# A streamed FFT filter and a Strassen-type gated projection on one core: where the sums of x's blocks, c22 and the filter step stand, which queue stores z, and when t is loaded

## Chip, core and metric

The kernel runs on one core of one Trainium2 chip. The metric is device time in microseconds (us) of one execution, given as the median of three runs. The engines are named as in the profile: PE is TensorE (its matmuls), PEld its weight loads, DVE VectorE, ACT ScalarE, POOL GpSimd, SP SyncE, which here does nothing but issue transfers.

## The reference

Two steps follow each other. `x` has 8 batches of 3072 tokens of 256 numbers, `d_ff` is 1536, all in f32.

```python
X = np.fft.rfft(x, axis=1)                     # along the 3072 tokens
y = np.fft.irfft(X * (filt_r + 1j * filt_i)[None], n=3072, axis=1)
t = y.reshape(8 * 3072, 256)
out = ((t @ w_a) * (t @ w_b)) @ w_out          # 256 -> 1536, 1536 -> 256
```

## The kernel before

**The two halves.** A main loop does the gated projection of batch b, and between its matmuls the Fourier filter of batch b+1 is streamed in. (The filter of batch 0 is done ahead of the loop, by the functions whose names begin with first_.) All matmuls on x's way take f32 numbers in two parts, a rounded part (xh, gh, yh, zh, ...) and the remainder (xl, gl, yl, zl), so that one product becomes three matmuls.

**The main loop.** A batch has 6 blocks c of 512 tokens, a block 6 pairs p of 256 columns of d_ff, so 36 pairs and 72 half pairs in a batch. A pair (function pair) forms both projections in 7 terms of 6 matmuls (term, L576 to L578) in place of 8, as Strassen's and Winograd's schemes do: sums of blocks of x and of the weights are multiplied, and sums of the terms give the blocks c11, c21, c22 and a21 of the result. The terms lie in the PSUM banks ps_p (two buffers, by turns from pair to pair), ps_q and ps_r. In program order: term 1 into ps_p, ScalarE copies it to s (L617); term 2 into ps_q, VectorE adds s and gives c11 (L621); term 5 into ps_r, copied to m5; term 6 on top of ps_p, copied to s; term 3 on top of ps_r, add with s gives c21 (L621); term 7 on top of ps_p, add with m5 gives c22 (L621); term 4 on top of ps_p again, from which a21 is copied (L654). Each of these overwrites or adds to a bank, and so waits for the copy or add that reads it. VectorE multiplies the two projections: L640 (c11 and c21), L645 (c22) and L655 (a21, straight from PSUM), into g. ScalarE casts g to gh (L584), GpSimd makes the remainder gl (L585), and the next pair multiplies both by w_out (project, L595 to L597, 24 matmuls in four places of the pair). A finished block is copied from PSUM and stored from the sync queue (store, L603). A pair has 42 + 24 = 66 matmuls.

**The hooks.** Twice in a pair, ahead of term 3 (half pair 2p) and ahead of term 4 (2p+1), `hooks` runs what a table, `plan`, names for this half pair. Its entries for a batch, by half pair, are:

- stage 1 of the next batch in 12 steps: load_x, load_s, split_x (L351, L352), s1 (6 matmuls at L360, then the cast zh L363 on ScalarE and the remainder zl L364 on VectorE), and store_z one half pair later (L369 to L372, issued from ScalarE's queue; a third store for the steps 8 to 11). One step every pair at half pairs up to 26; in batch 0 one step every half pair, from 12 on.
- the filter in 16 steps from half pair 29, one every pair: load_f and load_z (L391, L392, L398, from the sync queue, for the step after next), s2 (L407, L408; then on VectorE y at L418, two cross products at L420 into v, and y + v at L426), split_y (L433 on ScalarE, L434 on GpSimd) one half pair later, is1 (again L407, L408, copy to t, store to td from ScalarE's queue) three half pairs later.
- the last stage for the next block c+1: load_t (tt and gt, L531 and L533) at half pair 12c+2, is2 for each half of the columns (4 matmuls at L540, a copy to xf, L545) at 12c+4 and 12c+5, x_sums (four sums of x's blocks, L551) and x_parts (the casts xoh L560 and remainders xol L561) at 12c+6 and 12c+7. For the next batch's first block these are half pairs 65 to 70.

**What sets the order.** The program is scheduled by hand: each engine executes its instructions in the order of the code, and waits where its data or a buffer is not ready. s1, s2, is1 and is2 take by turns the two buffers of one PSUM pool (tag ff). Most SBUF tiles have one buffer: cs, g, s, m5, y, v, yh, yl, zh, zl, tt, gt and xf among them, so that the next use waits for the last reader of the use before. The core of a pair, from term 3 on:

```python
hooks(2 * p)
term(b, c, p, 3, rs)
add(1, rs, s)                         # c21, L621
nc.vector.tensor_tensor(out=g[:, 0]...)   # L640
term(b, c, p, 7, ps)
add(2, ps, m5)                        # c22, L621
...                                   # L645, project, parts
hooks(2 * p + 1)
term(b, c, p, 4, ps)
```

Of the kernel before, what the change touches and what calls it, by code (L numbers as in the profile page):

```python
# [14 lines left out]
ALU = mybir.AluOpType  # L15
# [181 lines left out]
def fft_filter_bilinear_kernel(ctx: ExitStack, tc, x, filt, fny, wa, wb, wo, s1c, gc, fc, fl, ic, sc, s1f, ff, fi, out):  # L197
# [168 lines left out]

    def store_z(b, i):
        zh, zl = held.pop(("zs", b, i))
        nc.scalar.dma_start(out=zd[b][0][:, 2 * i:2 * i + 2], in_=f32(zh))  # L369
        nc.scalar.dma_start(out=zd[b][1][:, 2 * i:2 * i + 2], in_=f32(zl))  # L370
        if i >= 8:
            nc.scalar.dma_start(out=zd[b][0][:, 2 * i + 8:2 * i + 10], in_=f32(zh))  # L372
# [39 lines left out]
    def s2(b, i):  # L412
        zt, fr, fm = held.pop(("z", b, i)), filts[2 * (i % 2)], filts[2 * (i % 2) + 1]
        ps = ps_f.tile([128, 2, D], F32, name="ps", tag="ff")
        turn(i, fct, flt, zt[:, 0], zt[0:96, 1], ps)
        y = later[0].tile([128, 2, D], F32, name="y", tag="y", bufs=1)
        v = later[0].tile([128, 2, D], F32, name="v", tag="v", bufs=1)
        nc.vector.scalar_tensor_tensor(out=y, in0=ps, scalar=sct[:, 0:1], in1=fr, op0=ALU.mult, op1=ALU.mult)  # L418
        for a in range(2):
            nc.vector.scalar_tensor_tensor(  # L420
                out=v[half[1 - a]], in0=ps[half[a]], scalar=sct[half[a], a:a + 1], in1=fm[half[1]],
                op0=ALU.mult, op1=ALU.mult,
            )
# [112 lines left out]
    def is2(b, c, k):  # L536
        tt, gt = held["t", b, c]
        ps = ps_f.tile([128, 4, N1], F32, name="ps", tag="ff")
        for n in range(4):
            nc.tensor.matmul(ps[:, n], tt[:, n, 128 * k:128 * k + 128], gt[:, n], start=True, stop=True)  # L540
        if k == 0:
            held["x", b, c] = moe[0].tile([128, 8, 256], F32, name="xf", tag="xf")
        else:
            del held["t", b, c]
        nc.scalar.copy(out=held["x", b, c][:, 2 * k:2 * k + 2].rearrange("p t n -> p (t n)"), in_=ps.rearrange("p n m -> p (n m)"))  # L545

    def x_sums(b, c):

        xf = held["x", b, c]
        for o, a, b_, op in ((4, 1, 0, ALU.subtract), (6, 3, 1, ALU.subtract), (5, 3, 4, ALU.subtract), (7, 2, 5, ALU.subtract)):  # L550
            nc.vector.tensor_tensor(out=xf[:, o], in0=xf[:, a], in1=xf[:, b_], op=op)  # L551

    def x_parts(b, c, part):
        xf = held["x", b, c]
        if part == 0:
            held["xo", b, c] = [p2.tile([128, 7, 256], F32R, name=t, tag=t) for t in ("xoh", "xol")]
        xh, xl = held["xo", b, c]
        for o, i in (((0, 1), (0, 1)), ((1, 3), (2, 4))) if part == 0 else (((3, 5), (4, 6)), ((5, 7), (6, 8))):
# [46 lines left out]
    def pair(u, last, hooks):  # L605

        b, c, p = u
        ps = ps_h.tile([128, 2, 256], F32, name="ps_p", tag="p", bufs=2)
# [11 lines left out]
        def add(n, bank, s):  # L620
            nc.vector.tensor_tensor(out=cs[:, :, n], in0=bank, in1=s, op=ALU.add)  # L621
# [15 lines left out]
        hooks(2 * p)  # L637
# [24 lines left out]


    with tc.manual_schedule():
# [53 lines left out]
        swap_front()  # L718
        is2(0, 0, 0)
        is2(0, 0, 1)  # L720
        x_sums(0, 0)
        x_parts(0, 0, 0)
        x_parts(0, 0, 1)

        last = None
        for b in range(B):
            plan = {}

            def at(slot, fn, *args):
                plan.setdefault(slot, []).append((fn, *args))  # L730
# [10 lines left out]
            if b + 1 < B:  # L741
# [89 lines left out]
```

## Time and profile before

| | us |
|---|---|
| runs | 2828.39, 2838.14, 2839.75 |
| median | 2838.14 |
| the profiled execution: time | 2827.78 |
| its span, first to last instruction | 2826.0 |
| PE busy in it | 2653.4 (94%) |
| DVE, ACT, POOL busy | 1755.6, 1409.0, 1401.5 (62, 50, 50%) |

Busy shares are means over the whole span, and its parts differ: the start and batch 0's stage 1 lie before 335 us, six batches between 335 and 2511 us, and from 2511 us on the last batch runs without a stream beside it. Matmuls overlap: a matmul's row lasts about 0.28 us, while one starts every 0.12 us. The granted clock is that of TensorE, as a share of full speed. A releaser in a row is what the profile infers to have ended a wait.

### The profile page before, as it was taken

How to read it: one execution, taken by the hardware profiler on the slowest of the kernel's cores; microseconds unless marked ns; L12 is line 12 of the kernel's file. 1: busy time of each engine (PE TensorE's matmuls, PEld its weight loads, DVE VectorE, ACT ScalarE, POOL GpSimd, SP SyncE). 2: the span in 40 equal slices, each digit the busy share in tenths (PEclk: the TensorE clock that was granted, in tenths of full speed). 3: DMA queues.
4: the chain of work that ended last, by engine and by line, in shares of the span. 5: the costliest groups of instructions: out<-in, count | busy, mean ns of one | idle time of the engine just before them, and what ended most of it. 6: DMA issues, size and time to landing. Idle time of an engine off the chain costs nothing.

```text
span 2826.0 us, 54174 instructions
## 1 busy us (share of the span) xinstructions
PE 2653.4 (94%) x20920; PEld 2541.0 (90%) x20920; DVE 1755.6 (62%) x2648; ACT 1409.0 (50%) x2630; POOL 1401.5 (50%) x1044
## 2 busy tenths in 40 slices
PE   4687899999999999999999999999999999999998
PEld 2387899998999999998999989999999999999998
DVE  5773576556855577455765567655785567754443
ACT  4443455554545555454555545555454545544443
POOL 3564454554544455454555545454464555544343
PEclk7889999999999999999999999999999999999999
DMA  7525342245413443244431445224441444310100
GB/s 241 160 89 170 120 149 85 79 140 148 134 47 133 139 125 114 74 139 124 135 113 64 137 136 147 64 98 159 122 127 47 146 135 127 109 31 20 38 20 16
DMA packets 213636, 310.89 MB, mean 110 GB/s; under 512 B 21393, under 2 KB 121298, under 8 KB 213330
## 3 DMA queue, kind: packets, MB, share of 16 engines
q1 hardware_dynamic: 156658, 227.46, 26.2%
q10 hardware_dynamic: 56720, 79.98, 8.3%
q8 instruction: 164, 2.69, 0.4%
q14 instruction: 94, 0.77, 0.1%
HBM read 202.49 MB, written 108.00 MB: 110 GB/s over the span
## 4 chain that ended last, share of the span: by engine, by line
PE 67%; DVE 21%; DMA 5%; issue 4%; ACT 2%; POOL 0%; SPq 0%; DVEq 0%; ACTq 0%; POOLq 0%
PE ps_p L576 8%; PE ps_p L578 7%; PE ps_p L577 7%; PE po L595 6%; PE po L597 6%; PE po L596 6%; DVE cs L621 6%; DVE g L640 4%; PE ps_r L576 4%; PE ps_r L578 4%; PE ps_r L577 4%; PE ps L540 3%; DVE xf L551 2%; DVE v L420 2%; PE ps_q L577 2%
## 5 line engine op out<-in xcount | busy, mean ns | idle before, releaser
L585 POOL TENSOR_TENSOR gl<-g,gh 128x512 fp32r<-128x512 f32 x576 | 784.8, 1362 | 1081.2 <-ACT gh L584 1038.6
L595 PE MATMUL po<-woh,gh 128*128 128x256 f32 x2304 | 650.1, 282 | 0.2 <-ACT gh L584 0.2
L596 PE MATMUL po<-wol,gh 128*128 128x256 f32 x2304 | 648.5, 281 | 0.0
L597 PE MATMUL po<-woh,gl 128*128 128x256 f32 x2304 | 647.4, 281 | 0.8 <-POOL gl L585 0.8
L584 ACT CAST gh<-g 128x512 fp32r<-128x512 f32 x576 | 358.1, 622 | 541.3 <-DVE g L640 380.3
L621 DVE TENSOR_TENSOR cs<-ps_r,s 128x512 f32<-128x512 f32 x288 | 198.9, 691 | 538.6 <-PE ps_r L578 502.8
L617 ACT COPY s<-ps_p 128x512 f32<-128x512 f32 x576 | 338.8, 588 | 317.3 <-PE ps_p L578 299.6
L597 PEld LDWEIGHTS po<-woh,gl 128*128 128x128 f32 x2304 | 437.2, 190 | 1.0 <-POOL gl L585 1.0
L595 PEld LDWEIGHTS po<-woh,gh 128*128 128x128 f32 x2304 | 436.6, 190 | 0.4 <-ACT gh L584 0.4
L596 PEld LDWEIGHTS po<-wol,gh 128*128 128x128 f32 x2304 | 435.8, 189 | 0.0
L576 PE MATMUL ps_p<-xoh,wah 128*128 128x256 f32 x1152 | 347.7, 302 | 70.1 <-DVE cs L621 50.5
L621 DVE TENSOR_TENSOR cs<-ps_q,s 128x512 f32<-128x512 f32 x288 | 199.2, 692 | 232.4 <-PE ps_q L578 210.8
L578 PE MATMUL ps_p<-xol,wah 128*128 128x256 f32 x1152 | 325.8, 283 | 0.3 <-POOL xol L561 0.3
L577 PE MATMUL ps_p<-xoh,wal 128*128 128x256 f32 x1152 | 325.7, 283 | 0.0
L576 PE MATMUL ps_p<-xoh,wbh 128*128 128x256 f32 x1152 | 325.5, 283 | 0.0
L577 PE MATMUL ps_p<-xoh,wbl 128*128 128x256 f32 x1152 | 324.9, 282 | 0.0
L578 PE MATMUL ps_p<-xol,wbh 128*128 128x256 f32 x1152 | 324.5, 282 | 0.0
L576 PEld LDWEIGHTS ps_p<-xoh,wah 128*128 128x128 f32 x1152 | 219.1, 190 | 111.8 <-DVE cs L621 92.3
L640 DVE TENSOR_TENSOR g<-cs 128x512 f32<-128x512 f32 x288 | 250.0, 868 | 32.8 <-POOL gl L585 2.6
L561 POOL TENSOR_TENSOR xol<-xf,xoh 128x256 fp32r<-128x256 f32 x192 | 246.5, 1304 | 17.5 <-ACT xoh L560 17.5
L434 POOL TENSOR_TENSOR yl<-y,yh 128x512 fp32r<-128x512 f32 x112 | 186.0, 1660 | 137.5 <-ACT yh L433 136.4
L578 PEld LDWEIGHTS ps_p<-xol,wah 128*128 128x128 f32 x1152 | 219.9, 191 | 0.6 <-POOL xol L561 0.6
(125 smaller groups left out, 6294.8 us busy)
## 6 DMA issues: line engine op xcount, KB each, us to landing
filt<-in_filt SPq DMA_DIRECT2D x336, 128.0 KB, 3.4
z<-zh ACTq DMA_DIRECT2D x112, 256.0 KB, 2.1
zt<-z SPq DMA_DIRECT2D x112, 256.0 KB, 3.1
td<-t ACTq DMA_DIRECT2D x128, 192.0 KB, 2.2
out<-ot SPq DMA_DIRECT2D x95, 256.0 KB, 2.1
tt<-td SPq DMA_DIRECT2D x47, 512.0 KB, 4.5
xt<-in_x SPq DMA_DIRECT2D x84, 256.0 KB, 2.8
st<-s1d SPq DMA_DIRECT2D x84, 256.0 KB, 3.5
```

What stands on the lines that cost most here:

```text
L561: nc.gpsimd.tensor_tensor(out=xl[:, o], in0=xf[:, i], in1=f32(xh[:, o]), op=ALU.subtract)
L576: nc.tensor.matmul(o, wh[:, p, w], xh[:, i], start=first and h == 0, stop=False, skip_group_check=True)
L577: nc.tensor.matmul(o, wl[:, p, w], xh[:, i], start=False, stop=False, skip_group_check=True)
L578: nc.tensor.matmul(o, wh[:, p, w], xl[:, i], start=False, stop=True, skip_group_check=True)
L584: nc.scalar.copy(out=gh, in_=g[:, f])
L585: nc.gpsimd.tensor_tensor(out=gl, in0=g[:, f], in1=f32(gh), op=ALU.subtract)
L595: nc.tensor.matmul(o, gh[:, ts], woh[:, n], start=n == 0 and j % 2 == 0, stop=False, skip_group_check=True)
L596: nc.tensor.matmul(o, gh[:, ts], wol[:, n], start=False, stop=False, skip_group_check=True)
L597: nc.tensor.matmul(o, gl[:, ts], woh[:, n], start=False, stop=n == NF - 1, skip_group_check=True)
L617: nc.scalar.copy(out=s, in_=bank)
L621: nc.vector.tensor_tensor(out=cs[:, :, n], in0=bank, in1=s, op=ALU.add)
L640: nc.vector.tensor_tensor(out=g[:, 0].rearrange("p (t n) -> p t n", t=2), in0=cs[:, 0, 0:2], in1=cs[:, 1, 0:2], op=ALU.mult)
```

## The change

1. **c22 first.** In pair the add of c22 stands ahead of the product L640 of before (L649 of after).
2. **Odd hooks.** hooks(2p+1) stand behind term 4 and its product (L661 of after), no longer ahead of term 4. The store at p = 1 stands behind term 6.
3. **The filter step in two places.** s2 keeps y and the first cross product. The second, the Nyquist row and y + v (sum_y) run in a new early hook, behind c11's add of the next pair.
4. **Sums of x's blocks.** x_sums is gone. is2 forms them: one operand is read from its PSUM bank, one in its first half, three in its second. is2 runs at half pairs 12c+5 and 12c+7, x_parts at 12c+8 and 12c+9 (for the next batch's first block 67, 69, 70, 71).
5. **t earlier.** load_t for a block runs at the half pair of the previous block's first x_parts, eight half pairs ahead of its is2; a batch's first block keeps two half pairs.
6. **z from the sync queue.** store_z issues on SyncE's queue. load_f goes one half pair later.

The diff, cut:

```diff
     def store_z(b, i):
-        nc.scalar.dma_start(out=zd[b][0][:, 2 * i:2 * i + 2], in_=f32(zh))
-        nc.scalar.dma_start(out=zd[b][1][:, 2 * i:2 * i + 2], in_=f32(zl))
+        nc.sync.dma_start(out=zd[b][0][:, 2 * i:2 * i + 2], in_=f32(zh))
+        nc.sync.dma_start(out=zd[b][1][:, 2 * i:2 * i + 2], in_=f32(zl))
...
         nc.vector.scalar_tensor_tensor(out=y, in0=ps, scalar=sct[:, 0:1], in1=fr, op0=ALU.mult, op1=ALU.mult)
-        for a in range(2):
-            nc.vector.scalar_tensor_tensor(
+        held["y", b, i] = y, v, ps, fm
+        cross(b, i, 0)
+
+    def sum_y(b, i):
+        cross(b, i, 1)
...
         nc.vector.tensor_tensor(out=y, in0=y, in1=v, op=ALU.add)
...
-    def x_sums(b, c):
+        for o, t, i in ((4, 1, 0),) if k == 0 else ((5, 1, 4), (6, 1, 1), (7, 0, 5)):
+            nc.vector.tensor_tensor(out=xf[:, o], in0=ps[:, t], in1=xf[:, i], op=ALU.subtract)
...
         add(0, qs, s)
+        hooks(early, 2 * p)
         term(b, c, p, 5, rs, True)
...
         add(1, rs, s)
+        term(b, c, p, 7, ps)
+        add(2, ps, m5)
         nc.vector.tensor_tensor(
...
-        term(b, c, p, 7, ps)
-        add(2, ps, m5)
...
         parts(u, 0)
-        hooks(2 * p + 1)
         term(b, c, p, 4, ps)
...
         nc.vector.tensor_tensor(out=g[:, 1, :256], in0=ps[:, 1], in1=a21, op=ALU.mult)
+        hooks(plan, 2 * p + 1)
...
                     at(t, s2, b + 1, i)
+                    early.setdefault(t + 1, []).append((sum_y, b + 1, i))
...
-                    t = 12 * c + 4 if c + 1 < NC else 67
-                    at(t - 2, load_t, nb, ncx)
+                    t = 12 * c + 5 if c + 1 < NC else 67
+                    if ncx == 0:
+                        at(t - 2, load_t, nb, 0)
                     at(t, is2, nb, ncx, 0)
-                    at(t + 1, is2, nb, ncx, 1)
-                    at(t + 2, x_sums, nb, ncx)
-                    at(t + 2, x_parts, nb, ncx, 0)
+                    at(t + 2, is2, nb, ncx, 1)
+                    if ncx + 1 < NC:
+                        at(t + 3, load_t, nb, ncx + 1)
+                    at(t + 3, x_parts, nb, ncx, 0)
```

VectorE's order in the middle of a batch, in a pair with a filter step, before (cs is written by the adds c21, c22 and, in the last row, c11 of the next pair):

```order
L621 TENSOR_TENSOR cs<-ps_r,s 128x2x256 [waits PE_49,Activation_49]
L640 TENSOR_TENSOR g<-cs 128x512 [waits DVE_49,Pool_49]
L621 TENSOR_TENSOR cs<-ps_p,m_15467 128x2x256 [waits PE_49]
L645 TENSOR_TENSOR g<-cs 128x256 [waits DVE_49]
L418 SCALAR_TENSOR_TENSOR y<-ps,sct,filt_93 128x512 [waits DMAHW6_49,DMAHW7_49,PE_49,Pool_49]
L420 SCALAR_TENSOR_TENSOR v<-ps,sct,filt_94 64x512 [waits DMAHW0_49]
L420 SCALAR_TENSOR_TENSOR v<-ps,sct,filt_94 64x512
L426 TENSOR_TENSOR y<-y,v 128x512 [waits DVE_49]
L655 TENSOR_TENSOR g<-ps_p,cs 128x256 [waits Activation_49]
L621 TENSOR_TENSOR cs<-ps_q,s 128x2x256 [waits DVE_49,PE_49,Activation_49]
```

And VectorE in the same place after:

```order
L627 TENSOR_TENSOR cs<-ps_r,s 128x2x256 [waits PE_49,Activation_49]
L627 TENSOR_TENSOR cs<-ps_p,m_19800 128x2x256 [waits PE_49]
L649 TENSOR_TENSOR g<-cs 128x512 [waits DVE_49,Pool_49]
L652 TENSOR_TENSOR g<-cs 128x256 [waits DVE_49]
L661 TENSOR_TENSOR g<-ps_p,cs 128x256 [waits Activation_49]
L418 SCALAR_TENSOR_TENSOR y<-ps,sct,filt_95 128x512 [waits DMAHW0_49,DMAHW7_49,PE_49,Pool_49]
L424 SCALAR_TENSOR_TENSOR v<-ps,sct,filt_96 64x512 [waits DMAHW1_49]
L627 TENSOR_TENSOR cs<-ps_q,s 128x2x256 [waits DVE_49,PE_49,Activation_49]
L424 SCALAR_TENSOR_TENSOR v<-ps,sct,filt_96 64x512
L434 TENSOR_TENSOR y<-y,v 128x512 [waits DVE_49]
```

c22's add moved up by one row, the product of a21 ahead of the filter's rows, and two of these behind c11's add of the next pair.

TensorE around the same s2 before, where po is the projection by w_out and ps_p the bank of terms 7 and 4:

```order
L597 MATMUL po<-woh,gl 128x256
L407 MATMUL ps<-zt,fct 128x512
L408 MATMUL ps<-zt,flt 128x512
L576 MATMUL ps_p<-xoh,wah 128x256
L577 MATMUL ps_p<-xoh,wal 128x256
```

And TensorE there after:

```order
L603 MATMUL po<-woh,gl 128x256
L582 MATMUL ps_p<-xoh,wah 128x256
L583 MATMUL ps_p<-xoh,wal 128x256
L584 MATMUL ps_p<-xol,wah 128x256
L582 MATMUL ps_p<-xoh,wbh 128x256
L583 MATMUL ps_p<-xoh,wbl 128x256
L584 MATMUL ps_p<-xol,wbh 128x256
L407 MATMUL ps<-zt,fct 128x512
L408 MATMUL ps<-zt,flt 128x512
```

s2's two matmuls moved from ahead of term 4 to behind it.

SyncE's queue between a batch's stage 1 and its first zt, before (after the last st load stand a block's stores, the filter's loads, t's and z's):

```order
L603 DMA out<-ot 128x512 [waits DMAHW0_49,Activation_49]
L391 DMA filt_93<-in_filt 64x512 [waits DMAHW1_49,DVE_49]
L391 DMA filt_93<-in_filt 64x512 [waits DMAHW3_49]
L392 DMA filt_94<-in_filt 64x512 [waits DMAHW5_49,DVE_49]
L391 DMA filt_95<-in_filt 64x512 [waits DMAHW7_49,DVE_49]
L391 DMA filt_95<-in_filt 64x512 [waits DMAHW0_49]
L392 DMA filt_96<-in_filt 64x512 [waits DMAHW1_49,DVE_49]
L531 DMA tt<-td 128x1024 [waits DMAHW2_49]
L533 DMA gt<-in_gc 128x512 [waits DMAHW3_49]
L398 DMA zt<-z_17797 128x2x256 [waits DMAHW6_49,DMAHW4_49]
```

And SyncE's queue there after:

```order
L609 DMA out<-ot 128x512 [waits DMAHW6_49,Activation_49]
L369 DMA z_13589<-zh 128x512 [waits DMAHW7_49]
L370 DMA z_13590<-zl 128x512 [waits DMAHW0_49,DVE_49]
L372 DMA z_13589<-zh 128x512 [waits DMAHW1_49]
L391 DMA filt_93<-in_filt 64x512 [waits DMAHW2_49]
L391 DMA filt_93<-in_filt 64x512 [waits DMAHW3_49]
L392 DMA filt_94<-in_filt 64x512 [waits DMAHW4_49]
L391 DMA filt_95<-in_filt 64x512 [waits DMAHW5_49]
L391 DMA filt_95<-in_filt 64x512 [waits DMAHW6_49]
L392 DMA filt_96<-in_filt 64x512 [waits DMAHW7_49]
L398 DMA zt<-z_13589 128x2x256 [waits DMAHW1_49,DMAHW0_49]
```

The last stage 1 step's three stores of z came in ahead of the filter's loads and the first zt, and tt and gt left this place.

## Rows read from the trace of the kernel before

**Rows 1.** The page's first part: engine, busy us, share of the span, instructions.

```profile
PE 2653.4 (94%) x20920; PEld 2541.0 (90%) x20920; DVE 1755.6 (62%) x2648; ACT 1409.0 (50%) x2630; POOL 1401.5 (50%) x1044
```

**Rows 2.** Stretch, us; busy (x) PE, PEld, DVE, ACT, POOL; clock; DMA share; GB/s.

```profile
210.00:335.00 125.00, 100.14 (x728) 95.90 (x727) 55.04 (x85) 50.20 (x98) 52.60 (x41) 0.90 0.46 150
```

**Rows 3.** The same view, a stretch in which TensorE does not wait.

```profile
1529.30:1539.60 10.30, 10.30 (x90) 10.30 (x89) 4.22 (x7) 5.58 (x10) 3.99 (x3) 1.00 0.47 159
```

**Rows 4.** Timeline of a pair without hook work: start, duration, instruction, [idle before <- releaser].

```profile
1516.44 0.69 DVE L621 TENSOR_TENSOR cs<-ps_r,s 128x512 f32<-128x512 f32 x1 [2.15 <-PE ps_r L578]
...
1517.85 0.68 DVE L621 TENSOR_TENSOR cs<-ps_p,m 128x512 f32<-128x512 f32 x1
...
1518.17 0.28 PE L597 MATMUL po<-woh,gl 128*128 128x256 f32 x1
...
1518.58 0.19 PEld L576 LDWEIGHTS ps_p<-xoh,wah 128*128 128x128 f32 x1 [0.33 <-DVE cs L621]
...
1518.82 0.28 PE L577 MATMUL ps_p<-xoh,wal 128*128 128x256 f32 x1
```

**Rows 5.** Waits of weight loads, 210 to 335 us: total, times, longest.

```profile
PEld ps_p L576 <- ACT s L617: 9.5, 4, 3.9
...
PEld ps L540 <- DMA tt<-td: 3.9, 1, 3.9
...
PEld ps_r L576 <- ACT m L617: 0.5, 1, 0.5
```

**Rows 6.** The same view, 335 to 2511 us.

```profile
PEld ps_p L576 <- DVE cs L621: 55.2, 109, 2.5
PEld ps_r L576 <- ACT m L617: 32.0, 50, 1.2
...
PEld ps L360 <- ACT xh L351: 0.2, 1, 0.2
```

**Rows 7.** The same view, 2511 to 2826 us.

```profile
PEld ps_p L576 <- DVE cs L621: 15.4, 31, 1.3
```

**Rows 8.** Timeline of a pair with a filter step.

```profile
1440.69 0.74 DVE L418 SCALAR_TENSOR_TENSOR y<-ps,sct,filt 128x512 f32<-128x512 f32 x1
...
1444.27 0.62 ACT L584 CAST gh<-g 128x512 fp32r<-128x512 f32 x1 [1.95 <-DVE g L655]
...
1445.42 0.38 PE L576 MATMUL ps_r<-xoh,wah 128*128 128x256 f32 x1 [0.43 <-ACT m L617]
```

**Rows 9.** Cast zh in batch 0; ScalarE's waits, 130 to 335; z's transfers.

```profile
222.99 0.59 ACT L363 CAST zh<-ps 128x512 fp32r<-128x512 f32 x1 [4.83 <-DMA z<-zh]
...
ACT zh L363 <- DMA z<-zh: 27.5, 9, 5.6
...
z<-zh ACTq DMA_DIRECT2D x112, 256.0 KB, 2.1
```

**Rows 10.** Matmuls' waits, 335 to 2511; a chain piece; the stretch behind it.

```profile
PE ps L540 <- DMA gt<-in_gc: 14.8, 7, 3.1
...
1637.34 5.89 DMA gt<-in_gc
...
1643.40:1647.60 4.20, 4.20 (x23) 4.20 (x24) 1.47 (x3) 0.59 (x1) 0.00 (x0) 0.60 0.24 54
```

**Rows 11.** Groups by line and shape: count, busy us, mean ns, idle before.

```profile
L551 DVE TENSOR_TENSOR xf<-xf 128x256 f32<-128x256 f32 x192 | 148.4, 811 | 16.1 <-ACT xf L545 14.4
L655 DVE TENSOR_TENSOR g<-ps_p,cs 128x256 f32<-128x256 f32 x288 | 122.1, 424 | 107.5 <-ACT cs L654 102.0
L561 POOL TENSOR_TENSOR xol<-xf,xoh 128x512 fp32r<-128x512 f32 x144 | 200.0, 1403 | 1.7 <-ACT xoh L560 1.7
L420 DVE SCALAR_TENSOR_TENSOR v<-ps,sct,filt 64x512 f32<-64x512 f32 x224 | 168.0, 750 | 5.2
L426 DVE TENSOR_TENSOR y<-y,v 128x512 f32<-128x512 f32 x112 | 86.9, 776 | 3.9
```

**Rows 12.** SyncE's issues ahead of a first zt.

```profile
1632.16 1.23 SPq L391 DMA_DIRECT2D filt<-in_filt  x2
```

More of the change, by code (lines that the diff above doesn't have):

```diff
@@ L368, in store_z @@
         zh, zl = held.pop(("zs", b, i))
[L369 to L370 removed]
+        nc.sync.dma_start(out=zd[b][0][:, 2 * i:2 * i + 2], in_=f32(zh))
+        nc.sync.dma_start(out=zd[b][1][:, 2 * i:2 * i + 2], in_=f32(zl))
         if i >= 8:
[L372 removed]
+            nc.sync.dma_start(out=zd[b][0][:, 2 * i + 8:2 * i + 10], in_=f32(zh))
     def load_tables():
@@ L418, in s2, with cross @@
         nc.vector.scalar_tensor_tensor(out=y, in0=ps, scalar=sct[:, 0:1], in1=fr, op0=ALU.mult, op1=ALU.mult)
-        for a in range(2):
-            nc.vector.scalar_tensor_tensor(
-                out=v[half[1 - a]], in0=ps[half[a]], scalar=sct[half[a], a:a + 1], in1=fm[half[1]],
-                op0=ALU.mult, op1=ALU.mult,
-            )
+        held["y", b, i] = y, v, ps, fm
+        cross(b, i, 0)
+    def cross(b, i, a):
+        _, v, ps, fm = held["y", b, i]
+        nc.vector.scalar_tensor_tensor(
+            out=v[half[1 - a]], in0=ps[half[a]], scalar=sct[half[a], a:a + 1], in1=fm[half[1]],
+            op0=ALU.mult, op1=ALU.mult,
+        )
+    def sum_y(b, i):
+        cross(b, i, 1)
+        y, v, ps, _ = held["y", b, i]
         if i == 0:
@@ L544, in is2 @@
             del held["t", b, c]
-        nc.scalar.copy(out=held["x", b, c][:, 2 * k:2 * k + 2].rearrange("p t n -> p (t n)"), in_=ps.rearrange("p n m -> p (n m)"))
-    def x_sums(b, c):
         xf = held["x", b, c]
-        for o, a, b_, op in ((4, 1, 0, ALU.subtract), (6, 3, 1, ALU.subtract), (5, 3, 4, ALU.subtract), (7, 2, 5, ALU.subtract)):
-            nc.vector.tensor_tensor(out=xf[:, o], in0=xf[:, a], in1=xf[:, b_], op=op)
+        ps = ps.rearrange("p (t n) m -> p t (n m)", t=2)
+        nc.scalar.copy(out=xf[:, 2 * k:2 * k + 2], in_=ps)
+        for o, t, i in ((4, 1, 0),) if k == 0 else ((5, 1, 4), (6, 1, 1), (7, 0, 5)):
+            nc.vector.tensor_tensor(out=xf[:, o], in0=ps[:, t], in1=xf[:, i], op=ALU.subtract)
     def x_parts(b, c, part):
@@ L557, in x_parts @@
         xh, xl = held["xo", b, c]
-        for o, i in (((0, 1), (0, 1)), ((1, 3), (2, 4))) if part == 0 else (((3, 5), (4, 6)), ((5, 7), (6, 8))):
+        for o, i in (((0, 1), (0, 1)), ((1, 3), (2, 4)), ((3, 5), (4, 6)), ((5, 7), (6, 8)))[2 * part:2 * part + 2]:
             o, i = slice(*o), slice(*i)
@@ L603, in store, with pair @@
         queue.dma_start(out=ov[:, 4 * c + 2 * h:4 * c + 2 * h + 2], in_=ot)
-    def pair(u, last, hooks):
+    def pair(u, last, plan, early, hooks):
         b, c, p = u
@@ L627, in pair @@
             parts(last, 1)
-            if p == 1 and c + b:
-                store(*before(b, c), 1, nc.sync)
         add(0, qs, s)
+        hooks(early, 2 * p)
         term(b, c, p, 5, rs, True)
@@ L636, in pair @@
             project(last, ((0, 0), (0, 1)))
-        hooks(2 * p)
+        if p == 1 and c + b:
+            store(*before(b, c), 1, nc.sync)
+        hooks(plan, 2 * p)
         term(b, c, p, 3, rs)
         add(1, rs, s)
+        term(b, c, p, 7, ps)
+        add(2, ps, m5)
         nc.vector.tensor_tensor(
@@ L720, in fft_filter_bilinear_kernel @@
         is2(0, 0, 1)
-        x_sums(0, 0)
         x_parts(0, 0, 0)
@@ L773, in fft_filter_bilinear_kernel, with hooks @@
                 if nb < B:
-                    t = 12 * c + 4 if c + 1 < NC else 67
-                    at(t - 2, load_t, nb, ncx)
-                    at(t, is2, nb, ncx, 0)
-                    at(t + 1, is2, nb, ncx, 1)
-                    at(t + 2, x_sums, nb, ncx)
-                    at(t + 2, x_parts, nb, ncx, 0)
-                    at(t + 3, x_parts, nb, ncx, 1)
+                    t = 12 * c + 5 if c + 1 < NC else 67
+                    if ncx == 0:
+                        at(t - 2, load_t, nb, 0)
+                    elif c == 0 and b == 0:
+                        at(0, load_t, 0, 1)
+                    at(t, is2, nb, ncx, 0)
+                    at(t + 2, is2, nb, ncx, 1)
+                    if ncx + 1 < NC:
+                        at(t + 3, load_t, nb, ncx + 1)
+                    at(t + 3, x_parts, nb, ncx, 0)
+                    at(t + 4, x_parts, nb, ncx, 1)
             for c in range(NC):
-                def hooks(f):
-                    for fn, *args in plan.get(NF * c + f, ()):
+                def hooks(of, f):
+                    for fn, *args in of.get(NF * c + f, ()):
                         fn(*args)
                 for p in range(NP):
-                    pair((b, c, p), last, hooks)
+                    pair((b, c, p), last, plan, early, hooks)
                     last = (b, c, p)
```

4 lines of the change are left out of this document (2 added, 2 removed).

## Prediction

> **What bounds the kernel now.** The page's first part comes first [rows 1]: TensorE is busy for 94% of the span. Where it is not, the stretches tell: from 210 to 335 us, in batch 0, it is busy for 100 of 125 us at a granted clock of 0.90 [rows 2]. The matmuls themselves cannot become fewer: in a stretch with no wait [rows 3] TensorE is busy for all of its 10.30 us, and neighbours start 0.12 us apart. So what can be won is the waiting, and I read it from the waits of the weight loads, because a matmul's own row lasts 0.28 us [rows 4] against a pitch of 0.12 and hides the first part of every wait. They sum to 29.1 us in six rows for 210 to 335 [rows 5] and to 106.0 in five for 335 to 2511 [rows 6]; in the last batch one row holds nearly all, 15.4 [rows 7].
>
> One wait costs a little more than its row. In [rows 4] the load waits 0.33 us, and the second matmul of the term starts at 1518.82, where two pitches behind 1518.17 are 1518.41: 0.41 us late, 0.08 more than the row. The clock adds to it: after a wait for gt it stood at 0.60 over 4.2 us, a mean of its two levels of 1.2 and 2.4 GHz [rows 10], so 0.4 x 4.2 = 1.7 us were lost.
>
> **c22 ahead of the products, and the hook behind term 4.** [rows 4] is a pair without hook work. VectorE adds c21 (L621 on ps_r), multiplies (L640), adds c22 (L621 on ps_p), and term 4, which overwrites the bank that this add reads, starts when it ends, at 1518.53. With c22 second, the add starts when c21's add (ended 1517.13) and term 7 are done, about 1517.2, and ends near 1517.9. TensorE could come at 1518.17 + 0.12 = 1518.29, so a wait of 0.33 becomes a slack of 0.4. That slack is the only cover left: today a hook's s1 (6 matmuls, 0.7 us) or s2 (0.5) stands ahead of term 4 and hides the wait; now it stands behind. So what delays VectorE's c21 add decides. The four sums of x's blocks (4 x 0.81 us, [rows 11]) leave that place. The second half of the filter step comes in behind c11's add: 0.68 + 0.75 + 0.78 = 2.2 us [rows 4, 11], between the ends of term 2 and term 3, in which TensorE runs 24 matmuls, 2.8 us, and mostly is1's 0.5. It fits. The rows on cs are 55.2 in 109 waits and 15.4 in 31 [rows 6, 7]; with 0.08 for each of 140 that is 82. I take four fifths, **66 us**, since a second releaser often stands close behind the first; the bounds are 30 (only the waits of pairs without hook work go) and 82.
>
> **The filter step's place.** In [rows 8] the filter's ops run from 1440.69 on, ahead of L655; the cast gh waits 1.95 us for L655, the copy m5 stands behind it on ScalarE's queue, and term 3 waits for m5. Now L655 stands ahead of them, and gh is ready when ScalarE reaches it. The row on m: 32.0 us in 50 waits [rows 6], with the 0.08 it is 36; I take **28**, bounds 10 and 36.
>
> **Sums of x's blocks from PSUM.** The trace has no such operation. Nearest row above: L551, the same sums from SBUF, 811 ns; nearest below: L655, the same size with one operand in PSUM, 424 ns [rows 11]. I take 424, since it shares the operands' kinds: four sums 1.7 us instead of 3.2. They now run in odd hooks behind L655, where TensorE does not wait for them; counted at nothing by itself. If that cover went, three of them (1.3 to 2.4 us) behind L655, y and v could push c11's add by 0.3 us or more.
>
> **t loaded ahead.** is2 waits for gt 7 times in 335 to 2511 us, 14.8 us, and once for tt before, 3.9 [rows 5, 10]. One such transfer took 5.89 us to land. Eight half pairs are some 35 us, so this goes, with 8 x 0.08 and up to 7 x 1.7 us of clock: 31. I take **29**, bounds 15 and 32. The first block of each next batch keeps its two half pairs; no wait of the trace lies there.
>
> **z from the sync queue.** ScalarE's cast into zh waits 4.83 us for the last z store to land [rows 9], because that store is issued from ScalarE's own queue just ahead of this cast. Such waits cost ScalarE 27.5 us, nine times, all in batch 0, where s1 comes every half pair. SyncE has only to wait for zl, so the store leaves about half a pair (4 us) earlier, more than its usual landing of 2.1 us [rows 9]. Of the 29.1 us in 210 to 335, 3.9 are tt's; 25 hang on this, and the clock of 0.90 costs up to 0.10 x 125 = 12 more. I take **26**, bounds 0 and 37.
>
> By the Trainium skill (DMA: Bandwidth & Descriptors, Issuing engines are not separate DMA queues) another issuing engine saves only the sequencer's issue time. By that alone this term would be 0 and the time 2732; the row speaks for a wait on landing, which an earlier issue shortens.
>
> **What the change costs.** SyncE takes 196 more issues, and its next load stands behind a wait for zl. The tight place is the first zt of a batch: the last three z stores and six filt loads go ahead of it (nine issues of about 0.6 us, [rows 12]), then some 5.9 us to land as for gt: 11 to 13 us behind the hook of half pair 26, where s2 now comes 96 matmuls, 11.3 us, behind it. That is 0 to 2 us and some clock, 1.2 x 7 = 8. At a batch's end x_parts moves one half pair later; two xol subtractions of 1.40 us [rows 11] behind gl reach the next batch's term 5 about 0.9 us late: 6. And s2's PSUM bank is held until c11's add of the next pair; where is2 takes the other bank, is1 may wait 0.2 us: 3. Together **17**, bounds 0 and 45.
>
> **Sum.** 66 + 28 + 29 + 26 - 17 = 132 us. The profiled execution took 2827.8 us (span 2826.0), so it would become 2696. It is close to the lowest of the three timed runs (2828.39); their median, 2838.14, less 132 is **2706 us**.
>
> **Rivals.**
> 1. *SyncE becomes the late queue.* The z stores hold up the loads behind them; the z term gives nothing and the first zt is 3 us late, with its clock loss, in each batch. For it: by these rows six filt issues alone take some 3.7 us [rows 12], and every load of a batch passes here. Against: a batch has about 156 issues in 330 us. Without the 26 and with 20 more of cost: 2752.
> 2. *The waits move instead of going.* The slack of 0.4 us is used up in pairs with s2, where hook work no longer covers it, so that half of the 66 and half of the 28 come back, 47, and half of z, 13: 2766. If t's gain alone is real, 2809.
> 3. *Nothing to measure.* The c22 add is released not by term 7 but by the copy m5, so the swap changes nothing, and the costs eat the rest: 2825 to 2850. Against: as the program stands, the add waits for TensorE alone.
> 4. *Slower: is1 waits for s2's bank.* VectorE now reads that bank until behind the next pair's c11 add. is1 usually takes the other bank, but if the pools' turn made all 112 is1 take this one and VectorE were late, the 132 would be gone from 1.2 us each on; at 2 us, 2706 + 224 = 2930. Against: VectorE is through with the bank about 1.6 us behind term 2, and is1 comes 18 matmuls, 2.1 us, behind it; VectorE must be 0.5 us late before it costs anything and 1.7 before it decides.
>
> **How the numbers follow.** The forecast's own range is 2670 to 2740: towards the terms' upper bounds at one end, z's lower bound at the other. Chances: forecast 0.64, rival 1 0.13, rival 2 0.12, rival 3 0.05, rival 4 0.06. The range takes in rival 1 and the half-way case of 2: 2670 to 2768, which leaves about 0.2 outside. Half a per cent of the time, 14 us, is about what a measurement of this kernel can tell from no change. Faster by more than that: 0.64 + 0.13 + 0.12 = 0.89; within it 0.05; slower 0.06.
>
> **What would show it.** In the waits of the weight loads from 335 us on, the row on cs should fall from 55 to about 15 and that on m from 32 to under 8; is2's wait for gt should be gone; a pair without hook work should last 0.4 us less. ScalarE's wait of zh for the store should fall from 27.5 to under 8 us, and the clock of batch 0's stretch rise above 0.93. The sums should show 0.42 to 0.5 us each. New rows to look for: s2 waiting for zt once a batch, is1 waiting for VectorE, xol in front of a batch's first term 5. The prediction is wrong if cs keeps more than half of its waits, or if a row on zt or on is1 appears above 20 us.

## The result and the profile after

The changed kernel takes 2685.43 us (median of 4 runs, 2684.15 to 2686.96); the kernel before took 2836.39 beside it (2828.39 to 2839.75). The ratio is 0.9472, 95% interval 0.9451 to 0.9493: 151 us less, where 132 were forecast (2706, range 2670 to 2768). The profiled execution took 2686.96 us, its span 2685.2, 140.8 less than before's. Beside the experiments below, in four later series, the kernel before took 2828.64 to 2830.32 (medians); against these the gain is 143 to 145 us. Its five medians lie up to 8 us apart, so a smaller difference between kernels of different series can't be told from none. Two of the kernels below had one slow execution each (sums from SBUF 3537.44 us at a clock of 0.665, three edits more 4222.50 at 0.555), and their times are the medians of the other three.

The page's first part of the kernel after (engine, busy us, share, instructions; before in [rows 1]):

```profile
PE 2590.9 (96%) x20920; PEld 2521.5 (94%) x20920; DVE 1667.8 (62%) x2648; ACT 1411.5 (53%) x2630; POOL 1321.5 (49%) x1044
```

The waits of the weight loads of after from 335 us to the end (total us, times, longest), which answer to [rows 6, 7]:

```profile
PEld po L603 <- POOL gl L591: 7.5, 22, 0.9
PEld ps_r L584 <- POOL xol L567: 3.9, 7, 0.6
PEld ps L405 <- DMA zt<-z: 0.3, 1, 0.3
```

Of more than 120 us of waiting 11.7 are left, and none of the rows on cs, m and gt. The pair without hook work, in after's timeline, answers to [rows 4] (start, duration, instruction, [idle before <- releaser]):

```profile
1407.90 0.69 DVE L627 TENSOR_TENSOR cs<-ps_r,s 128x512 f32<-128x512 f32 x1 [2.15 <-PE ps_r L584]
...
1408.54 0.69 DVE L627 TENSOR_TENSOR cs<-ps_p,m 128x512 f32<-128x512 f32 x1
...
1409.14 0.68 DVE L649 TENSOR_TENSOR g<-cs 128x512 f32<-128x512 f32 x1
...
1409.63 0.28 PE L603 MATMUL po<-woh,gl 128*128 128x256 f32 x1
...
1409.75 0.28 PE L582 MATMUL ps_p<-xoh,wah 128*128 128x256 f32 x1
```

c22's add runs right behind c21's and ends at 1409.23, and term 4 follows the projection by 0.12 us, TensorE's pitch. The slack, the time between the two, is 0.52 us.

Batch 0's stage 1 did less well. Its stretch (us; busy and count of PE, PEld, DVE, ACT, POOL; clock; DMA share; GB/s) answers to [rows 2]:

```profile
210.00:335.00 125.00, 106.87 (x841) 104.57 (x840) 63.91 (x103) 56.70 (x108) 55.86 (x44) 0.96 0.50 160
```

And ScalarE's wait of the cast zh, 130 to 335 us, to [rows 9]:

```profile
ACT zh L363 <- DMA z<-zh: 29.2, 9, 5.1
```

The wait that the new queue was to take away stands at 29.2 us, with 27.5 before.

To place the gains I take the start of term 2 in each batch's first pair from the profiled execution of each kernel. By it, in us:

| | ahead of batch 0 | batch 0 | batches 1 to 6 | batch 7 to the end |
|---|---|---|---|---|
| before | 130.9 | 383.2 | 1996.4 | 315.5 |
| c22 first, alone | 130.3 | 379.1 | 1948.9 | 299.1 |
| t early, alone | 131.5 | 376.5 | 1973.1 | 316.9 |
| after | 131.6 | 356.1 | 1898.9 | 298.6 |
| after, sums as before | 131.2 | 368.1 | 1926.0 | 299.3 |
| after, with three edits more (last experiment) | 130.6 | 331.7 | 1895.6 | 297.9 |

### The profile page after: what moved, and what is told of

It is laid out like the page before. It is cut to its first block, busy times and chain, and to the rows that moved or that the text cites. A ratio compares the mean times of both kernels' runs of the same rounds, so it can differ in the third digit from the quotient of the medians.

```text
span 2685.2 us, 54082 instructions
## 1 busy us (share of the span) xinstructions
PE 2590.9 (96%) x20920; PEld 2521.5 (94%) x20920; DVE 1667.8 (62%) x2648; ACT 1411.5 (53%) x2630; POOL 1321.5 (49%) x1044
## 4 chain that ended last, share of the span: by engine, by line
PE 87%; POOL 4%; DVE 3%; DMA 3%; issue 2%; ACT 1%; SPq 0%; ACTq 0%; POOLq 0%; DVEq 0%
PE po L603 10%; PE ps_p L582 9%; PE ps_p L584 9%; PE ps_p L583 9%; PE po L601 9%; PE po L602 9%; PE ps_r L584 5%; PE ps_r L582 5%; PE ps_r L583 5%; PE ps L548 3%; PE ps_q L582 2%; PE ps_q L584 2%; PE ps_q L583 2%; PE ps L360 2%; PE ps L407 2%
## 5 line engine op out<-in xcount | busy, mean ns | idle before, releaser
L591 POOL TENSOR_TENSOR gl<-g,gh 128x512 fp32r<-128x512 f32 x576 | 748.4, 1299 | 959.0 <-ACT gh L590 891.1
L601 PE MATMUL po<-woh,gh 128*128 128x256 f32 x2304 | 656.9, 285 | 0.0
L582 PE MATMUL ps_p<-xoh,wah 128*128 128x256 f32 x1152 | 326.9, 284 | 29.9 <-ACT s L623 16.5
L649 DVE TENSOR_TENSOR g<-cs 128x512 f32<-128x512 f32 x288 | 301.3, 1046 | 5.6 <-POOL gl L591 5.6
L661 DVE TENSOR_TENSOR g<-ps_p,cs 128x256 f32<-128x256 f32 x288 | 122.1, 424 | 213.9 <-ACT cs L660 211.2
L442 POOL TENSOR_TENSOR yl<-y,yh 128x512 fp32r<-128x512 f32 x112 | 144.2, 1288 | 223.8 <-ACT yh L441 223.8
```

The costliest lines, as they stand in the source:

```text
L582: nc.tensor.matmul(o, wh[:, p, w], xh[:, i], start=first and h == 0, stop=False, skip_group_check=True)
L591: nc.gpsimd.tensor_tensor(out=gl, in0=g[:, f], in1=f32(gh), op=ALU.subtract)
L601: nc.tensor.matmul(o, gh[:, ts], woh[:, n], start=n == 0 and j % 2 == 0, stop=False, skip_group_check=True)
L649: nc.vector.tensor_tensor(out=g[:, 0].rearrange("p (t n) -> p t n", t=2), in0=cs[:, 0, 0:2], in1=cs[:, 1, 0:2], op=ALU.mult)
```

## The experiments

### One part alone, in the kernel before

The kernel before ran beside these at 2830.1 us.

**z from the sync queue, alone:** all three stores.

```diff
-        nc.scalar.dma_start(out=zd[b][0][:, 2 * i:2 * i + 2], in_=f32(zh))
+        nc.sync.dma_start(out=zd[b][0][:, 2 * i:2 * i + 2], in_=f32(zh))
...
```

> The kernel before with one edit: the stores of z are issued from the sync queue. Theory of the prediction (the store only has to wait for zl there, so it leaves half a pair earlier): 26 us less, about 2810, and ScalarE's wait of the cast zh for the store in batch 0 falls from 27.5 us to under 8. Rival, from the trace of the changed kernel, in which that wait is still 29.2 us: on the sync queue the store stands behind load_x, which waits for the remainder xl, which waits on ScalarE and GpSimd behind the cast zh itself; a closed chain. Then the time is 2828 to 2840, no change, and the wait stays above 20 us.

2826.46 us, ratio 0.9994 (0.9981 to 1.0006): no change. The rival holds (its time was 2828 to 2840, counted from 2836). ScalarE's wait in its trace, 130 to 335 us:

```profile
ACT zh L363 <- DMA z<-zh: 26.8, 8, 6.6
```

**c22 first, alone.**

```diff
-        nc.vector.tensor_tensor(out=g[:, 0]...
-        term(b, c, p, 7, ps)
-        add(2, ps, m5)
+        term(b, c, p, 7, ps)
+        add(2, ps, m5)
+        nc.vector.tensor_tensor(out=g[:, 0]...
```

> The kernel before with one edit: the add of c22 stands ahead of the product L640; the hooks stay ahead of term 4. Theory of the prediction: the add is released by term 7, not by the copy m5, so the waits of ps_p for the adds (55.2 + 15.4 us of weight loads, 82 with the recovery) mostly go: 2836 - 66 = 2770, and 2754 to 2806 by the bounds. The last batch alone falls by 15 to 17 us, a pair without hook work from 8.17 to 7.77. Rival (the copy m5 releases the add): no change, 2836.

2761.83 us, ratio 0.9758 (0.9742 to 0.9775): 68 us, and in the table 16.4 of them in the last batch. A pair without hook work takes 7.77 us. The waits of its weight loads from 335 us on:

```profile
PEld ps_r L576 <- ACT m L617: 38.9, 76, 0.9
...
PEld ps_p L576 <- DVE cs L621: 9.7, 11, 1.4
```

The row on cs fell from 70.6 us (55.2 and 15.4, [rows 6, 7]) to 9.7. The row on m rose from 32.0 in 50 waits to 38.9 in 76, as if a part of that wait had been hidden behind the other.

**c22 first and the odd hooks behind term 4,** the filter step still in one piece.

```diff
         parts(u, 0)
-        hooks(2 * p + 1)
         term(b, c, p, 4, ps)
...
         nc.vector.tensor_tensor(out=g[:, 1, :256], in0=ps[:, 1], in1=a21, op=ALU.mult)
+        hooks(2 * p + 1)
```

> The kernel before with two edits: c22's add ahead of the product, and the odd hooks behind term 4 and its product; the filter step stays in one piece, the sums of x's blocks read SBUF. Theory of the prediction: the hook's new place gives the waits of ps_r for m5 back, 28 us more than the swap alone (2742). Rival: the four sums and the whole filter step now stand between the product of a21 and the next pair's c11 add, and hold that up; then it is no better than the swap alone, 2760 to 2780, with waits for ps_p or ps_q on L621 in the pairs with a filter step.

2803.62 us, ratio 0.9907 (0.989 to 0.9924): 42 us slower than the swap alone, worse than the rival said. The waits of its weight loads from 335 us on:

```profile
PEld ps_p L576 <- ACT s L617: 73.2, 85, 1.9
...
PEld ps_r L576 <- ACT m L617: 1.9, 3, 0.8
```

The wait for m5 goes, as the prediction reads it, and a larger one comes: term 7 waits for the copy s. Why is seen below, in the filter step in one piece. Seven of the 85 waits, 1.9 us each, stand at a batch's end, where the odd hook (half pair 69) holds the four sums: a batch's last pair takes 9.73 us here and 7.92 with the swap alone. That is 13 of the 42.

**t early, alone.**

```diff
-                    at(t - 2, load_t, nb, ncx)
+                    if ncx == 0:
+                        at(t - 2, load_t, nb, 0)
+                    elif c == 0 and b == 0:
+                        at(0, load_t, 0, 1)
...
                     at(t + 2, x_sums, nb, ncx)
+                    if ncx + 1 < NC:
+                        at(t + 2, load_t, nb, ncx + 1)
```

> The kernel before with one edit: tt and gt of a block are loaded ten half pairs ahead of its is2, behind the previous block's sums (a batch's first block keeps two). Theory of the prediction: the waits for gt (14.8 us, 7 times) and tt (3.9 us) go, with the clock lost behind them: 29 us less, 2807, bounds 2804 to 2821. Rival: the zt and filt loads that stood in the same queue are the late ones once t is out of the way, and s2 waits instead: 2825 or more.

2798.27 us, ratio 0.9885 (0.9864 to 0.9906): 32 us. No row on gt or tt is left in its waits of 335 us and later. The load stands ten half pairs ahead of its is2 here, and nine in the changed kernel, not the eight of its description (seven in both for a batch's second block).

### One part undone, in the kernel after

These compare with 2685.4 us, which was measured in a series of its own.

**z from ScalarE's queue again.** The three lines of the first diff, turned back.

> The changed kernel with one part undone: z stored from ScalarE's queue again. Theory of the prediction: 26 us more, 2711. Rival (the store on the sync queue hangs on load_x, so it won nothing in batch 0): 2680 to 2693, the same within 8 us.

2690.22 us, 4.8 more, which is within what two series differ by. With 3.6 by the medians in the kernel before, where the interval takes in no change, z's queue is worth 0 to 5 us and not 26. The stretch of batch 0, in the columns of [rows 2], is close to that of after (106.9 us busy, clock 0.96):

```profile
210.00:335.00 125.00, 106.04 (x817) 103.52 (x816) 60.94 (x98) 55.40 (x107) 55.32 (x43) 0.93 0.49 157
```

**The filter step in one piece.**

```diff
         cross(b, i, 0)
+        sum_y(b, i)
...
-                    early.setdefault(t + 1, []).append((sum_y, b + 1, i))
```

> The changed kernel with one part undone: the second cross product, the Nyquist row and y + v follow the first cross product in s2 again, ahead of the next pair's c11 add. By the prediction's reading the whole step is 0.74 + 2 x 0.75 + 0.78 = 3.0 us on VectorE behind the product of a21, and the c11 add comes 0.5 to 1.5 us late in each of 112 filter steps; what waits for it is term 3 (the bank ps_r is not touched by c11, but c21's add and with it term 7 and 4 are). If the slack of 0.4 us is all there is: 0.5 us in each of 112, 2685 + 56 = 2741. Rival: VectorE catches up before term 4, so that it costs under 10 us.

2745.98 us: 60.6 more. The waits of its weight loads from 335 us on:

```profile
PEld ps_p L583 <- ACT s L624: 60.2, 81, 1.1
```

Its timeline in one filter step (start, duration, instruction, [idle before <- releaser]):

```profile
1313.86 0.74 DVE L418 SCALAR_TENSOR_TENSOR y<-ps,sct,filt 128x512 f32<-128x512 f32 x1
...
1314.63 1.51 DVE L425 SCALAR_TENSOR_TENSOR v<-ps,sct,filt 64x512 f32<-64x512 f32 x2
...
1316.18 1.09 DVE L435 TENSOR_TENSOR y<-y,v 128x512 f32<-128x512 f32 x1
1317.31 0.69 DVE L628 TENSOR_TENSOR cs<-ps_q,s 128x512 f32<-128x512 f32 x1
1318.09 0.58 ACT L624 COPY s<-ps_p 128x512 f32<-128x512 f32 x1 [1.83 <-DVE cs L628]
...
1318.72 0.19 PEld L583 LDWEIGHTS ps_p<-xoh,wah 128*128 128x128 f32 x1 [0.72 <-ACT s L624]
```

The whole step stands ahead of c11's add. That add is late, and s has one buffer: the second copy into s waits 1.83 us for it, and term 7, which overwrites what this copy reads, 0.72 us. The split takes 1.5 us or more out of this way, behind the add.

**The odd hooks ahead of term 4 again,** with the split kept.

```diff
         parts(u, 0)
+        hooks(plan, 2 * p + 1)
         term(b, c, p, 4, ps)
...
-        hooks(plan, 2 * p + 1)
```

> The changed kernel with one part undone: the odd hooks stand ahead of term 4 and its product again (c22 first, the filter step in two places and all else kept). Theory of the prediction (its term for the hook's place): the waits of ps_r for the copy m5 come back, 28 us, 2713. Rival: the split alone has already halved what stands ahead of the product of a21 (0.74 + 0.75 us instead of 3.0), so that the place of the hook is worth under 10 us once the split is there: 2685 to 2695.

2690.22 us, 4.8 more, again no more than two series differ by: the rival. Its waits have no row on m5. Once the step is in two places, it matters little on which side of the product of a21 the first half stands.

**The sums of x's blocks, both operands from SBUF, in the new place.**

```diff
-            nc.vector.tensor_tensor(out=xf[:, o], in0=ps[:, t], in1=xf[:, i], op=ALU.subtract)
+            nc.vector.tensor_tensor(out=xf[:, o], in0=xf[:, 2 * k + t], in1=xf[:, i], op=ALU.subtract)
```

> The changed kernel with the sums of x's blocks formed in the same place, both operands from SBUF. Prediction's estimate: 811 against 424 ns, four sums 1.5 us longer in 47 blocks, counted at nothing by itself since TensorE does not wait for VectorE there: 2685 to 2690. Rival: three sums of 0.8 us push the c11 add and with it term 4: 0.5 to 1 us in each of 47, 2708 to 2732.

2688.17 us, 2.7 more: no change that can be told. Its sums by line (count, busy us, mean ns), from the execution at a clock of 0.665:

```profile
L557 DVE TENSOR_TENSOR xf<-xf 128x256 f32<-128x256 f32 x192 | 76.5, 440 | 68.4 <-ACT xf L555 68.3
```

VectorE's durations don't follow TensorE's clock: L418 is 744 ns there and 742 in after. What runs beside a sum may: 7 of these 192 have an operation of GpSimd beside them, and 25 of the 192 in after. The same sums from SBUF that took 811 ns in [rows 11] take 440 here. So the place is enough to make most of them short. Whether the PSUM operand matters for the few that meet GpSimd in this place at full clock, no trace shows.

**The sums in their old place and form,** t still early; is2 and x_parts go back with them.

```diff
-        for o, t, i in ((4, 1, 0),) if k == 0 else ((5, 1, 4), (6, 1, 1), (7, 0, 5)):
-            nc.vector.tensor_tensor(out=xf[:, o], in0=ps[:, t], in1=xf[:, i], op=ALU.subtract)
...
+    def x_sums(b, c):
...
-                    t = 12 * c + 5 if c + 1 < NC else 67
+                    t = 12 * c + 4 if c + 1 < NC else 67
...
-                    at(t + 2, is2, nb, ncx, 1)
+                    at(t + 1, is2, nb, ncx, 1)
+                    at(t + 2, x_sums, nb, ncx)
...
+                    at(t + 2, x_parts, nb, ncx, 0)
+                    at(t + 3, x_parts, nb, ncx, 1)
```

> The changed kernel with one part undone: the sums of x's blocks in one piece from SBUF, with the places of before (is2 at half pairs 12c+4 and 12c+5, the four sums at 12c+6 in an even hook, x_parts at 12c+6 and 12c+7); t is still loaded early. The swap of c22, t and z, measured alone or undone, leave some 45 of 150 us to the filter step's two places and to the sums. Prediction (the sums are worth nothing by themselves): 2681 to 2690, where the earlier x_parts give back up to 4 us. Rival (four sums of 0.81 us ahead of c21's add eat the slack, and the busy first pairs of batch 0 more so): 0.25 to 0.6 us in each of 47 blocks and up to 12 us in batch 0, 2697 to 2725.

2726.05 us: 40.6 more, 1 us above the rival's range. The waits of its weight loads from 335 us on:

```profile
PEld ps_p L584 <- DVE cs L629: 21.0, 23, 1.8
PEld ps_p L584 <- ACT s L625: 13.3, 7, 1.9
```

The first row belongs to the blocks within a batch, where the sums stand in an even hook (12c+6) ahead of c21's add. The second is a batch's end, seven times, where they stand in an odd hook (69) ahead of c11's add. (The row on xol, 3.9 us in after, is gone, since x_parts comes earlier here.) The table puts 27 of the 41 in batches 1 to 6 and 12 in batch 0. A batch's end in the timeline:

```profile
1452.13 4.52 DVE L559 TENSOR_TENSOR xf<-xf 128x256 f32<-128x256 f32 x4
1452.58 2.36 POOL L569 TENSOR_TENSOR xol<-xf,xoh 128x256 fp32r<-128x256 f32 x2
...
1456.58 0.68 DVE L629 TENSOR_TENSOR cs<-ps_q,s 128x512 f32<-128x512 f32 x1
1457.35 0.58 ACT L625 COPY s<-ps_p 128x512 f32<-128x512 f32 x1 [2.56 <-DVE cs L629]
...
1457.98 0.19 PEld L584 LDWEIGHTS ps_p<-xoh,wah 128*128 128x128 f32 x1 [1.90 <-ACT s L625]
```

The four sums take 4.52 us beside GpSimd's remainder xol, c11's add is late, and by the same chain as above term 7 waits 1.90 us. That pair, a batch's last, lasts 9.73 us, and 7.78 in after. With c22 first alone, the odd hooks still ahead of term 4, it lasts 7.92: at a batch's end it is the sums and the hooks' new place together that cost.

**The second half of is2 one half pair earlier,** so that the three sums stand in an even hook.

```diff
-                    at(t + 2, is2, nb, ncx, 1)
+                    at(t + 1, is2, nb, ncx, 1)
```

> The changed kernel with the second half of is2 one half pair earlier, in an even hook ahead of term 3, so that three sums (3 x 0.42 us) and the copy ahead of them stand in front of c21's add on VectorE. If the sums' place is a term that the prediction left out: the add comes 0.6 + 1.3 us behind is2 where term 3 takes 0.7, so 1.2 late, less 0.4 of slack, 0.8 us in each of 47 blocks: 2685 + 38 = 2723. Rival (neighbouring pairs of the kernel before were only 0.25 us longer with four sums there): under 12 us, 2685 to 2697.

2719.85 us, 34.4 more, near the 38 of the first theory. With sums of 0.42 us that read PSUM, the place of these sums and of the copy ahead of them costs this much: the row on cs is back in the waits of its weight loads from 335 us on:

```profile
PEld ps_p L582 <- DVE cs L627: 26.6, 44, 1.0
```

### What still held batch 0

The trace of after shows why the new queue did not help. One step of stage 1 (timeline, 228 to 236 us):

```profile
228.81 0.58 ACT L363 CAST zh<-ps 128x512 fp32r<-128x512 f32 x1 [2.31 <-DMA z<-zh]
...
229.29 0.62 ACT L351 CAST xh<-xt 128x512 fp32r<-128x512 f32 x1
229.43 0.69 DVE L364 TENSOR_TENSOR zl<-ps,zh 128x512 fp32r<-128x512 f32 x1 [2.47 <-ACT zh L363]
...
229.99 1.31 POOL L352 TENSOR_TENSOR xl<-xt,xh 128x512 fp32r<-128x512 f32 x1 [2.42 <-ACT xh L351]
...
231.33 0.38 SPq L339 DMA_DIRECT2D xt<-in_x  x1
...
231.76 0.46 SPq L369 DMA_DIRECT2D z<-zh  x1
...
235.19 0.59 ACT L363 CAST zh<-ps 128x512 fp32r<-128x512 f32 x1 [1.91 <-DMA z<-zh]
```

zl is ready at 230.12. The store leaves at 231.76, because load_x stands ahead of it on SyncE and waits for a free buffer of xt, until the remainder xl ends at 231.30. xl waits for xh, and xh stands on ScalarE behind the cast zh, which waits for the store of the step before. The chain closes at 6.4 us a step.

**Three buffers for xt,** so that load_x waits for no step just before.

```diff
-        xt = later[0].tile([128, 2, D], F32, name="xt", tag="xt", bufs=2)
+        xt = later[0].tile([128, 2, D], F32, name="xt", tag="xt", bufs=3)
```

> The changed kernel with three buffers for the load of x instead of two, so that load_x no longer waits for the remainder xl of the step just before, and the z store behind it on the sync queue leaves at once. If that chain (cast zh, cast xh, remainder xl, load_x's issue, z store, next cast zh; some 6.4 us a step) is what holds batch 0's stage 1, the wait of zh falls from 29.2 to under 10 us and batch 0 gets 8 to 20 us shorter: 2665 to 2677. Rival: the landing of the store (3.4 us on this queue) or ScalarE's and VectorE's other work in batch 0 bounds the step anyway: 2681 to 2688.

2670.33 us, 15.1 less than after: the chain it was. The wait of zh fell by more than half, but not to the 10 us expected.

ScalarE's wait of the cast zh, 130 to 335 us, in its trace:

```profile
ACT zh L363 <- DMA z<-zh: 11.3, 5, 4.7
```

The longest of the 5 waits left is one store that left just behind tt and gt and took 6.85 us to land.

**Three edits that the traces point to.** Beside xt's third buffer, zh and zl by turns in two buffers (zl shares with yl as zh with yh), and is2 of a next batch's first block two half pairs earlier, for the 3.9 us of xol.

```diff
-        zh = later[0].tile([128, 2, D], F32R, name="zh", tag="zh", bufs=1)
+        zh = later[0].tile([128, 2, D], F32R, name="zh", tag=("zh", "yh")[i % 2], bufs=1)
...
-                    t = 12 * c + 5 if c + 1 < NC else 67
+                    t = 12 * c + 5 if c + 1 < NC else 65
```

> The changed kernel with three edits meant to take away what still waits in its trace: three buffers for the load of x; zh and zl by turns in two buffers (they borrow yh's and yl's, which stage 1 leaves idle), so that no cast waits for a store's landing; is2 of the next batch's first block two half pairs earlier, so that its last remainder xol no longer reaches the next batch's first pair late (8.39 us instead of 7.77, seven times, 4.3 us). If the wait of zh (11.3 us still with three buffers of x) and xol are what is left: 2670 - 8 - 4 = 2658, and the wait of zh is under 3 us. Rival: the 20 us of batch 0's first pairs and the DMA queue bound batch 0, and the step of stage 1 is late for its loads instead: 2666 to 2672.

2656.89 us, ratio to the kernel before 0.9387 (0.9369 to 0.9405): 28.5 us, one per cent, below the changed kernel. Batch 0 takes 331.7 us in place of 356.1, and no row of zh waiting for a store is left. The stretch from 210 to 335 us, in the columns of [rows 2]:

```profile
210.00:335.00 125.00, 124.91 (x1036) 123.53 (x1035) 82.73 (x129) 70.84 (x133) 67.20 (x52) 1.00 0.56 183
```

## Why the prediction came out

The range held and the sum was 19 us short of the 151, or 13 of the 145 by which after lies below the 2830.1 that stood beside the single edits. Of its five terms two were right, one was right in its row but can't be told apart in the times, and two were wrong. That the sum came so near is in part luck: z was 21 to 26 too high, the costs were 13 too high, and the filter step and the sums together 12 to 17 too low.

- **c22 ahead of the products: 66 said, 68 measured alone.** The reading of [rows 4] is confirmed: term 7 releases the add, and four fifths was a fair share of the row.
- **t early: 29 said, 32 measured alone.** The rows on gt and tt, 18.7 us, are gone; the rest fits the clock's part of the sum (up to 7 x 1.7 us, an estimate from [rows 10]), which no run took by itself.
- **The filter step's place: 28 said.** The row on m is gone, 32.0 us before. But the step named two edits as one and gave the credit to the wrong one. The split does it: undone, it costs 60.6. The hook's place is worth 0 to 5 once the split is there, and without the split and with the sums as before it costs 42. How much the split, the hook's place and the sums bring together is what is left of the 145: less 68, 32 and 0 to 5 (z) that is 40 to 45 us, if the parts add up; 28 + 0 was said of them. How it divides can't be read off. Undone one at a time, split and sums cost 61 and 41, together more than twice of it, since each was undone with the hooks already moved: the 13 us at the batches' ends in the 41 make good what the hook's move would have cost there.
- **The sums: nothing said, up to 41 measured.** The step that failed is "where TensorE does not wait for them; counted at nothing by itself". The new place was judged rightly, the old one was not: for all blocks but a batch's first it was the even hook, ahead of c21's add, and had its own price (34 us, with sums of 0.42 us put there in the changed kernel), which I charged to cs alone. And 811 ns was a mean of two kinds. The instruction's view of L551, minimum, median and maximum:

```profile
L551 DVE TENSOR_TENSOR xf<-xf x192: 408/426/1523, 126.8 to 2746.0; 128x256 f32<-128x256 f32 x192
```

  Half of them take 408 to 426 ns, others up to 1523. In the trace, 83 of the 192 take 700 ns or more, and each of these has an operation of GpSimd beside it for over half of its time, as in the 4.52 us above. The other 109 take 428 ns at most, and 40 of these have GpSimd as much beside them. What divides the two is the order: in all 83 GpSimd's operation began before the sum, and the sum ended 278 to 289 ns behind the end of that operation; in the 40 it began with the sum or behind it (at most 3 ns ahead). The product of a21, with one operand in PSUM, stays at 410 to 427 in after, though each of the 288 has an operation of GpSimd beside it, gl for 266 of them:

```profile
L661 DVE TENSOR_TENSOR g<-ps_p,cs x288: 410/425/427, 141.7 to 2675.5; 128x256 f32<-128x256 f32 x144
```

  By the Trainium skill (SBUF — State Buffer, section SBUF: two separate sides) a VectorE operation with two SBUF inputs and a GpSimd operation take one shared port pair by an exclusive lock, and the later one waits for the whole of the other. These rows agree, by the order above, and 1523 ns is the sum's own 0.41 us and 1.11 of waiting, less than one remainder of 1.3 us.
- **z from the sync queue: 26 said, 0 to 5 measured.** The step that failed is "SyncE has only to wait for zl, so the store leaves about half a pair (4 us) earlier". A queue was looked at for what the moved store waits for, and not for what stands ahead of it: load_x, held by the same chain. That the cast waits for the landing was right, as the 15 us of a third xt buffer show, and the 24 by which batch 0 fell with two buffers of zh as well. The rule quoted there from the Trainium skill (DMA: Bandwidth & Descriptors, Issuing engines are not separate DMA queues) gave 0 for this term. The result agrees, but by another mechanism, since stores that do leave earlier, with the third buffer of xt, gain.
- **What the change costs: 17 said, about 4 measured.** xol at a batch's start is there, 3.9 us where 6 were said. s2 waits for the first zt for 0.3 us in all, and no clock was lost (1.00 over 335 to 2511 us); is1 waits for no bank. Rivals 2 to 4 have no row in the trace. Of rival 1 the half about z came true, the other way round, since here a load (load_x) held up the stores; the half about zt did not.

Batch 0 fell by 27 us although z gave next to nothing: t brought 6.7 and c22 4.1 of it by the single edits, and undoing the sums takes 12 back. That the stretch of [rows 2] went from 100 to 107 busy us and its clock from 0.90 to 0.96 therefore doesn't speak for z: with z on ScalarE's queue again it holds 106 at 0.93.

What stays open is how the 40 to 45 us divide between the split and the sums, since neither was run alone in the kernel before.

## What to carry to other kernels

When an instruction moves to another queue, list what stands ahead of it there and what that waits for; a load that waits for a buffer can close a loop through the very wait that the move was to end. An in-order engine's work is best placed by the add or copy behind it that frees a single buffer: here VectorE's lateness at c11 reached TensorE through the one buffer of s. And before a mean duration is used as a price, look at its minimum and maximum: a mean of two kinds names neither.

## What the runs showed of the hardware

- A 128x256 VectorE subtraction of two SBUF operands took 408 to 1523 ns (median 426) in before, 700 or more only where a GpSimd operation had begun before it (83 of 192, each ending 278 to 289 ns behind that operation's end). Where GpSimd began with it or behind it, it took 428 ns at most. A product of that size with an operand in PSUM took 410 to 427 ns in after, with GpSimd at work beside all 288.
- Stores of z from the sync queue, with a load of x issued just ahead, landed in 3.4 us (231.76 to 235.12, after). From ScalarE's queue in batch 0 of before, 8 of 14 landed in 2.0 to 2.5 and the others in up to 5.3. Behind tt and gt one took 6.85 (three buffers for xt).
- TensorE's granted clock in the 125 us of batch 0's stretch was 0.90 in before (100.1 us busy), 0.96 in after (106.9) and 1.00 with the last three edits (124.9).
